# Largest value over the partitions: from a transpose and a product on TensorE to a reduction on GpSimd, and biases turned by transfers

## The chip, the cores and the metric

The kernel runs on one core of a Trainium2 chip. The core has TensorE (matmuls, from SBUF into PSUM banks), VectorE, ScalarE, GpSimd, and SyncE, whose queue (SP) issues most DMA transfers. Each engine works through its own queue in order, and engines wait for each other by semaphores. The metric is the device time of one execution, in microseconds (us). Before the change the median of 3 runs is 686.72 us (685.91 to 687.05).

## The reference, cut to what matters

The input x has 2048 rows of 1024, in bf16. Two branches read it, and a gate mixes their outputs.

```
qkv = x @ wqkv                     # 32 heads of 32; each row attends to 8 rows, 2 apart
a   = softmax(q.k / sqrt(32)) v @ wo
z   = gelu(x @ w_in)               # 3584 columns
z1, z2 = z[:, :1792], layernorm(z[:, 1792:])
g   = w_sp @ z2 + b_sp[:, None]    # w_sp is 2048 x 2048, b_sp has 2048 entries
b   = (z1 * g) @ w_out
out = s * a + (1 - s) * b          # s = sigmoid(x . gate_w)
```

## The kernel before, in words

All matmuls are in 16 bits, most of them 128x128 weights against 512 moving columns (L302, L617, L802, L829, L920, L1048, L1137). Their order on TensorE is: the second half of x @ w_in (`z2_tile`, L302), the q, k, v blocks (`plain_rows`, L617, then `row_pair`, L637), the rest of the second half (L302 again), the first half of x @ w_in (L802), w_sp @ z2 (`g_chunk`, L829, then `seven_products`, L920), and the products with w_out and wo (`mix_pair`, `attn_pair` and `both_pairs`, L1048, L1127, L1137). The attention itself is elementwise work on VectorE (L342 to L398), laid beside the matmuls. ScalarE copies most results out of the PSUM banks (L307, L623, L805, L833). The tile called `ps` rotates through all eight banks, and the small results `po` and `pt` of this change take banks from the same rotation.

The order of the work is written out by hand. The class `Beat` counts the matmul columns issued so far and turns them into a time; functions are put on a list with a due time (`beat.at`) and are issued when the count of columns reaches it. So the order in each engine's queue is fixed when the kernel is built.

Parts of four products (`row_pair`, `seven_products`, `mix_pair` and `both_pairs`) combine blocks of their factors in fp16 and use seven block products in place of eight. For that, factors are first multiplied by a power of two that brings their largest value to a known size, and results are multiplied by the inverse. The generator `whole_power` (L494) finds such a power for a whole matrix. It is given the largest absolute value of each partition (`top`, 128 x 1) and has three steps, issued at three places of the order:

1. VectorE raises `top` to a floor (L496), cuts it down to its power of two (L497, L498) and writes it as bf16 (L499).
2. TensorE turns the 128 values into one row (L503), and VectorE takes the largest of the row (L504).
3. TensorE multiplies a column of ones with this value spread over 512 columns (L506), which puts it on all partitions. VectorE copies it out (L507), makes the scaling power `up1` and its inverse `back` with integer operations on the exponent (L508 to L512), and multiplies `factors` by the inverse (L513).

`whole_power` is used seven times: for x (first step at L552, the others from L695), q (L595, L716), w_out (`w_steps`, L771 and L1276), wo (`wo_steps`, L1278 and L1277), the attention output (`o_steps`, L1233 to L1236), the first half of z1 * g (`v_steps`, L1227 to L1231) and the second half (`u_steps`, L1296, L1177, L1193). The x scale is read by ScalarE at L561 and by VectorE at L562, in `x_block_sums`.

The rows of the second half of w_sp have powers of their own (`row_powers`, L850), which read the biases of these rows too, one row per partition. So b_sp's second half must lie as `b_in`, 128 partitions by 8. Before the change it is loaded as 8 rows of 128 (`b_row`, L738), transposed on TensorE (`biases`, L786) and copied by ScalarE (L787). The scaled biases `b_up` (L866) go the other way: a product with the identity on TensorE (L871), a copy by ScalarE (L873), a store to `bsp_d` in DRAM (L874). Later L877 loads them from there onto all partitions, for `seed` (L775), which puts biases into the banks before the products are added.

Of the kernel before, what the change touches and what calls it, by code (L numbers as in the profile page):

```python
# [2 lines left out]

# [7 lines left out]
F32 = mybir.dt.float32  # L11
BF = mybir.dt.bfloat16
F16 = mybir.dt.float16
I32 = mybir.dt.int32

P = 128
# [41 lines left out]
def kernel(  # L58
# [13 lines left out]
    nc = tc.nc  # L72
# [4 lines left out]
    sm = ctx.enter_context(tc.tile_pool(name="small", bufs=1))  # L77
    psum = ctx.enter_context(tc.tile_pool(name="psum", bufs=8, space=bass.MemoryType.PSUM))
# [15 lines left out]
    bsp_d = dpool.tile([8, P], BF, name="bsp_d")  # L94

    ones = nc.const_aps.tensor(1.0, [P, 512], BF)
# [6 lines left out]
    ident = sm.tile([P, P], BF, name="ident")  # L103
# [15 lines left out]
    expo = sm.tile([P, 8], I32, name="expo")  # L119
    up = sm.tile([P, 8], I32, name="up")  # L120
    down = sm.tile([P, 8], I32, name="down")
    b_row = sm.tile([8, P], BF, name="b_row")
    b_in = sm.tile([P, 8], BF, name="b_in")
    b_up = sm.tile([P, 8], BF, name="b_up")
    w_l1 = sm.tile([P, 7], F32, name="w_l1")
# [1 line left out]
    u_l1 = sm.tile([P, NF], F32, name="u_l1")  # L127
    top = sm.tile([P, 1], F32, name="top")
    top_i = sm.tile([P, 1], I32, name="top_i")
    top_b = sm.tile([P, 1], BF, name="top_b")  # L130
    top_1 = sm.tile([1, 1], BF, name="top_1")
    wo_l1 = sm.tile([P, 4], F32, name="wo_l1")
    o_l1 = sm.tile([P, 32], F32, name="o_l1")
    wo_up = sm.tile([P, 1], I32, name="wo_up")
# [97 lines left out]
    sync = nc.sync  # L232
# [250 lines left out]
    def load_w1(ch):  # L483
        ncol = min(512, FH - 512 * ch)
        sync.dma_start(w1_slots[ch % 2][:, :, 0:ncol], win_v[:, :, 512 * ch:512 * ch + ncol])
# [5 lines left out]
    def load_z1c(c):  # L491
        sync.dma_start(z1c_slots[c][:, 0:12, :].rearrange("p f t -> p (f t)"), z1_d[c, :, 0:12 * 512])

    def whole_power(up1, factors):  # L494
        v = nc.vector
        v.tensor_scalar(top[:], top[:], TINY, None, ALU.max)  # L496
        v.tensor_scalar(top_i[:], top[:].bitcast(I32), 23, None, ALU.logical_shift_right)  # L497
        v.tensor_scalar(top_i[:], top_i[:], 23, None, ALU.logical_shift_left)  # L498
        v.tensor_copy(top_b[:], top_i[:].bitcast(F32))  # L499
        yield  # L500
        po = psum.tile([P, 512], F32, name="po", tag="ps")
        pt = po[0:1, 0:P // 2].bitcast(BF)
        nc.tensor.transpose(pt, top_b[:], ident[:])  # L503
        v.tensor_reduce(top_1[:], pt, AX.X, ALU.max)  # L504
        yield
        nc.tensor.matmul(po[:], ones[0:1, 0:P], top_1[:].to_broadcast([1, 512]), start=True, stop=True)  # L506
        v.tensor_copy(top[:], po[:, 0:1])  # L507
        v.tensor_scalar(top_i[:], top[:].bitcast(I32), 23, None, ALU.logical_shift_right)  # L508
        v.tensor_scalar(up1[:], top_i[:], -1, 254 + TOP, ALU.mult, ALU.add)
        v.tensor_scalar(up1[:], up1[:], 23, None, ALU.logical_shift_left)  # L510
        v.tensor_scalar(back[:], top_i[:], -TOP, None, ALU.add)
        v.tensor_scalar(back[:], back[:], 23, None, ALU.logical_shift_left)  # L512
        v.tensor_scalar(factors, factors, back[:].bitcast(F32), None, ALU.mult)  # L513
        yield
# [30 lines left out]
    for i in range(2, 16):  # L545
        x_sum(i)
        z2_tile(i, 0)
        if i == 8:
            sync.dma_start(z2_d[:], z2[:, 4:8, 0:2, :])
    nc.vector.tensor_reduce(top[:], x_l1, AX.X, ALU.max)  # L550
    x_steps = whole_power(x_up, q_back[:])
    next(x_steps)  # L552

# [26 lines left out]
    def q_sum(k):  # L580
# [8 lines left out]
        beat.on_vector(1.3)  # L589

    q_steps = whole_power(q_up, q_back[:])

    def q_first_step():
# [141 lines left out]

    load_w1(0)
    load_w1(1)
    sync.dma_start(b_row[:], bass.AP(tensor=B_b_sp.tensor, offset=B_b_sp.offset + 1024, ap=[[P, 8], [1, P]]))  # L738
    for i in range(2, 16):
        z2_tile(i, 1)  # L740
        if i == 3:
# [26 lines left out]
    for g in range(NG):  # L768
        beat.at(beat.now + 6.0 + 10.0 * g, lambda g=g: turn_wo(g))
    w_steps = whole_power(w_up, omg[:])  # L770
    beat.at(beat.now + 72.0, lambda: (nc.vector.tensor_reduce(top[:], w_l1[:], AX.X, ALU.max), next(w_steps)))  # L771

    seeded = []

    def seed(v):  # L775
        ps = psum.tile([P, 512], F32, name="ps", tag="ps")
        nc.scalar.copy(ps[:], v)
        seeded.append(ps)
# [2 lines left out]
        seed(bsp_bc[:, 1024:1536])  # L781
        seed(bsp_more)

    def biases():
        pt = psum.tile([P, 8], BF, name="pt", tag="ps")
        nc.tensor.transpose(pt[:], b_row[:], ident[0:8, 0:8])  # L786
        nc.scalar.copy(b_in[:], pt[:])  # L787

    for f in range(NF):
        ch = f // 4  # L790
        w1 = w1_slots[ch % 2]
        if f % 4 == 0 and ch in (1, 2):
            load_w1(ch + 1)
        z1s = z1s_slots[f % 4]
        if f == 4:
            biases()
        for c in range(4):
            if 4 * f + c >= 4 * NF - AHEAD:
                seed(bsp_bc[:, 0:512])
            ps = psum.tile([P, 512], F32, name="ps", tag="ps")  # L800
            for kt in range(KT):
                nc.tensor.matmul(ps[:], w1[:, kt, (f % 4) * P:(f % 4 + 1) * P], xT[:, kt, 512 * c:512 * (c + 1)],  # L802
                                 start=(kt == 0), stop=(kt == KT - 1))
            keep = f > 11 and c < 2
            nc.scalar.activation(z1c_slots[c][:, f, :] if keep else z1s[:, c, :], ps[:], ACT.Gelu_apprx_tanh)  # L805
            beat.run(KT * 512)
        c0 = 2 if f > 11 else 0
        beat.at(beat.now + (3.0 if f < 11 else 0.0), lambda f=f, c0=c0, z1s=z1s: sync.dma_start(
            z1_d[c0:4, :, f * 512:(f + 1) * 512].rearrange("c p t -> p c t"), z1s[:, c0:4, :]))
        if f == 12:  # L810
            load_z1c(0)
# [55 lines left out]
        TT(omg[:, 8:16], omg[:, 8:16], down[:].bitcast(F32), ALU.mult)  # L867

    def scaled_biases():
        pt = psum.tile([8, 512], F32, name="pt", tag="ps")  # L870
        nc.tensor.matmul(pt[:].rearrange("p (a t) -> p a t", a=4), b_up[:],  # L871
                         ident[:].rearrange("p (a t) -> p a t", a=1).to_broadcast([P, 4, P]), start=True, stop=True)
        nc.scalar.copy(b_row[:], pt[:, 0:P])  # L873
        sync.dma_start(bsp_d[:], b_row[:])  # L874

    def load_scaled_biases():
        sync.dma_start(bsp_bc[:, 1024:S], bass.AP(tensor=bsp_d.tensor, offset=bsp_d.offset, ap=[[0, P], [1, 1024]]))  # L877
# [388 lines left out]
    beat.at(t0 + 41.5, lambda: row_powers(4, 8))  # L1266
    beat.at(t0 + 42.5, row_powers_back)
    beat.at(t0 + 64.0, scaled_biases)
    beat.at(t0 + 76.0, load_scaled_biases)
    for k in range(2):  # L1270
# [60 lines left out]
```

## Time and profile before

| what | value |
|---|---|
| median of 3 runs | 686.72 us |
| the profiled execution's own time | 685.84 us |
| its span | 683.7 us |
| L503, transpose, 7 times | 217 ns each, from 39.5 to 588.9 us |
| L506, product, 7 times | 384 ns each, from 42.4 to 595.4 us |
| L786 / L871, biases on TensorE, once each | 174 / 379 ns |
| mean of a 512-column matmul (L829) | 379 ns |
| GpSimd, busy in all | 13.2 us, 9.3 of it in four pows (L470) |

The profile is one execution, taken by the hardware's profiler; its span leaves out some 2 us around the kernel. Rows of a timeline give the start and the length of a group of equal instructions, the engine (PE is TensorE, PEld its weight loads, DVE VectorE, ACT ScalarE, POOL GpSimd, SPq the queue of SP), the line, and what is written from what; in brackets stands how long the engine was idle before it and who ended that. Matmuls overlap: a row's length is longer than the distance from one start to the next.

### The profile page before, as it was taken

The page shows a single profiled execution, that of the slowest core. Times are in us where ns is not written, and L with a number is a line of the kernel's source. Part 1 is how long each engine was busy: PE and PEld are TensorE (multiplying, and loading weights), DVE is VectorE, ACT ScalarE, POOL GpSimd, SP SyncE. Part 2 cuts the span into 40 slices and gives each one's busy share as a digit, 9 for nine tenths or more (in the row PEclk, how much of TensorE's full clock was granted, in tenths as well). Part 3 has the DMA queues.
Part 4 walks back from the last instruction along what each step waited for, and adds up shares of the span by engine and source line. Part 5 has one row for each costly group of instructions (what it writes and reads, how often), then busy time and mean ns, then how long its engine had stood idle before and what let it go on. Part 6 is the DMA issues. An engine that isn't in the chain of part 4 may idle for free.

```text
span 683.7 us, 8977 instructions
## 1 busy us (share of the span) xinstructions
PE 676.1 (99%) x3276; PEld 355.4 (52%) x3327; DVE 564.2 (83%) x701; ACT 417.1 (61%) x767; POOL 13.2 (2%) x45
## 2 busy tenths in 40 slices
PE   9999999999999999999999999999999999999997
PEld 4489666666654565444444444444444444444443
DVE  4649959999999998999998889895578888766653
ACT  4358767655556999758854896426977442232322
POOL 0000000000000022000000000000000000000000
PEclk9999999999999999999999999999999999999999
DMA  8995975544697308899877958919211513222210
GB/s 233 176 206 156 201 206 149 157 127 96 163 234 221 142 1 208 176 285 360 272 297 251 246 204 218 241 46 285 84 57 37 154 37 87 63 68 70 65 45 32
DMA packets 187996, 108.67 MB, mean 159 GB/s; under 512 B 146480, under 2 KB 172592, under 8 KB 187696
## 3 DMA queue, kind: packets, MB, share of 16 engines
q1 hardware_dynamic: 186224, 101.81, 56.6%
q10 hardware_dynamic: 1728, 6.29, 2.6%
q8 instruction: 26, 0.43, 0.3%
q14 instruction: 18, 0.15, 0.1%
HBM read 59.51 MB, written 34.41 MB: 137 GB/s over the span
## 4 chain that ended last, share of the span: by engine, by line
PE 97%; DMA 1%; issue 0%; SPq 0%; ACT 0%; DVE 0%; DVEq 0%
PE ps L617 16%; PE ps L829 14%; PE ps L802 14%; PE ps L302 14%; PE ps L920 12%; PE ps L1048 12%; PE ps L637 7%; PE ps L1137 6%; PE ps L1127 1%; DMA arena<-in_B_w_in_dram 1%; PE po L506 0%; SPq L523 0%; PE po L503 0%; SPq L521 0%; SPq L519 0%
## 5 line engine op out<-in xcount | busy, mean ns | idle before, releaser
L617 PE MATMUL ps<-arena 128*128 128x512 bf16 (+1 forms) x637 | 115.6, 337 | 0.2
L302 PE MATMUL ps<-arena 128*128 128x512 bf16 (+1 forms) x501 | 97.3, 352 | 0.7
L829 PE MATMUL ps<-arena 128*128 128x512 bf16 x439 | 97.3, 379 | 0.5
L617 PEld LDWEIGHTS <-arena 128*128 128x128 bf16 x640 | 83.1, 144 | 27.8 <-issue 0.5
L802 PE MATMUL ps<-arena 128*128 128x512 bf16 x439 | 96.6, 379 | 0.5
L1048 PE MATMUL ps<-arena 128*128 128x512 f16 (+1 forms) x380 | 91.2, 379 | 0.5
L920 PE MATMUL ps<-arena 128*128 128x512 f16 (+1 forms) x385 | 84.9, 379 | 0.6 <-issue 0.3
L302 PEld LDWEIGHTS <-arena 128*128 128x128 bf16 x512 | 50.2, 98 | 47.5 <-issue 0.6
L802 PEld LDWEIGHTS <-arena 128*128 128x128 bf16 x448 | 43.7, 98 | 52.4
L348 DVE TENSOR_TENSOR arena<-arena 128x8192 bf16<-128x8192 bf16 x16 | 70.7, 4420 | 0.2
L391 DVE TENSOR_TENSOR arena<-arena,att_A 128x8192 bf16<-128x8192 bf16 x16 | 70.7, 4419 | 0.0
L829 PEld LDWEIGHTS <-arena 128*128 128x128 bf16 x448 | 43.4, 98 | 52.5 <-issue 0.5
L1048 PEld LDWEIGHTS <-arena 128*128 128x128 f16 (+1 forms) x392 | 38.3, 98 | 46.1
L920 PEld LDWEIGHTS <-arena 128*128 128x128 bf16 (+1 forms) x392 | 38.0, 98 | 46.1 <-issue 0.5
L623 ACT CAST arena<-ps 128x512 bf16<-128x512 f32 (+1 forms) x80 | 38.9, 527 | 32.2 <-PE ps L617 30.6
L351 DVE TENSOR_TENSOR arena<-arena 128x4096 bf16<-128x4096 bf16 (+1 forms) x32 | 56.2, 1755 | 0.8
L637 PE MATMUL ps<-arena 128*128 128x512 f16 (+1 forms) x224 | 52.4, 379 | 0.0
L307 ACT ACTIVATE arena<-ps 128x512 bf16<-128x512 f32 x64 | 34.2, 537 | 27.8 <-PE ps L302 27.8
L1137 PE MATMUL ps<-arena 128*128 128x512 f16 (+3 forms) x200 | 50.3, 375 | 0.1
L1117 DVE SCALAR_TENSOR_TENSOR arena<-ps,g_s,arena 128x512 bf16<-128x512 f32 (+2 forms) x33 | 24.0, 734 | 28.7 <-ACT arena L1169 19.9
L805 ACT ACTIVATE arena<-ps 128x512 bf16<-128x512 f32 x56 | 32.1, 600 | 19.8 <-PE ps L802 17.5
L637 PEld LDWEIGHTS <-arena 128*128 128x128 f16 (+1 forms) x224 | 32.2, 144 | 16.1
(204 smaller groups left out, 779.1 us busy)
## 6 DMA issues: line engine op xcount, KB each, us to landing
arena<-k_d SPq DMA_DIRECT2D x8, 960.0 KB, 7.3
arena<-v_d SPq DMA_DIRECT2D x8, 960.0 KB, 6.5
arena<-in_A_wqkv_dram SPq DMA_DIRECT2D x24, 256.0 KB, 5.1
z_d<-arena SPq DMA_DIRECT2D x12, 512.0 KB, 7.6
arena<-q_d SPq DMA_DIRECT2D x8, 512.0 KB, 3.9
o_d<-arena SPq DMA_DIRECT2D x4, 1024.0 KB
arena<-in_B_w_in_dram SPq DMA_DIRECT2D x4, 1024.0 KB
arena<-in_B_w_sp_dram ACTq DMA_DIRECT2D x8, 512.0 KB, 6.7
```

Source lines behind the costliest of these rows:

```text
L302: nc.tensor.matmul(ps[:, 0:N], xT[:, kt, i * P:(i + 1) * P], w2[c][:, kt, 0:N], start=(kt == 0), stop=(kt == KT - 1))
L348: TT(prod.rearrange("p (w j c) -> p w j c", w=W, j=8, c=C), in0, in1, ALU.mult)
L351: return lambda: TT(pv[:, :, 0:half], pv[:, :, 0:half], pv[:, :, half:2 * half], ALU.add)
L391: TT(prod.rearrange("p (w j d h) -> p w j d h", w=W, j=8, d=DH, h=HG), in0, in1, ALU.mult)
L617: nc.tensor.matmul(ps[:, n0:n1].rearrange("p (t c) -> p t c", c=C), lhsT, wgt[:, pos0:pos1, kt, :], start=(kt == 0), stop=(kt == KT - 1))
L623: nc.scalar.copy(slot[:, j % 4, n0:n1], ps[:, n0:n1])
L637: nc.tensor.matmul(dst[:].rearrange("p (t c) -> p t c", c=C), lhs(k), rhs[:, :, k, :], start=first and k == 0, stop=k == 3, skip_group_che ...
L802: nc.tensor.matmul(ps[:], w1[:, kt, (f % 4) * P:(f % 4 + 1) * P], xT[:, kt, 512 * c:512 * (c + 1)], start=(kt == 0), stop=(kt == KT - 1))
L829: nc.tensor.matmul(ps[:], z2[:, f, i, :], wsp[:, i, :, :].rearrange("p a t -> p (a t)"), start=False, stop=(i == 15), skip_group_check=True)
L920: nc.tensor.matmul(dst[:], lhs[:, k, :], rhs(k), start=False, stop=k == 7, skip_group_check=True)
L1048: nc.tensor.matmul(dst[:], lhs[:, j, :], rhs(j), start=first and j == 0, stop=j == 6, skip_group_check=not first)
L1137: nc.tensor.matmul(dst, lhs[:, k, :], rhs[:, k, :], start=first and k == 0, stop=k == 3, skip_group_check=not first)
```

## The change

In `whole_power` the maximum over the partitions is now one GpSimd instruction, `partition_all_reduce`, issued in the first step. It reads `top` in float32 and writes the largest value to all partitions of `top_all`. The bf16 cut, the transpose, the row maximum, the product and the copy go. The three steps stay where they were, the second of them empty, and the last one starts from `top_all`.

The biases are turned by the transfers: `b_in` is loaded in its final layout, element by element, and the scaled biases are stored to `bsp_d` element by element from `b_up`. `biases` and its call go, and `scaled_biases` is one DMA.

```diff
-    b_row = sm.tile([8, P], BF, name="b_row")
...
-    top_b = sm.tile([P, 1], BF, name="top_b")
-    top_1 = sm.tile([1, 1], BF, name="top_1")
+    top_all = sm.tile([P, 1], F32, name="top_all")
...
         v.tensor_scalar(top[:], top[:], TINY, None, ALU.max)
-        v.tensor_scalar(top_i[:], top[:].bitcast(I32), 23, None, ALU.logical_shift_right)
-        v.tensor_scalar(top_i[:], top_i[:], 23, None, ALU.logical_shift_left)
-        v.tensor_copy(top_b[:], top_i[:].bitcast(F32))
+        nc.gpsimd.partition_all_reduce(top_all[:], top[:], P, bass_isa.ReduceOp.max)
         yield
-        po = psum.tile([P, 512], F32, name="po", tag="ps")
-        pt = po[0:1, 0:P // 2].bitcast(BF)
-        nc.tensor.transpose(pt, top_b[:], ident[:])
-        v.tensor_reduce(top_1[:], pt, AX.X, ALU.max)
         yield
-        nc.tensor.matmul(po[:], ones[0:1, 0:P], top_1[:].to_broadcast([1, 512]), start=True, stop=True)
-        v.tensor_copy(top[:], po[:, 0:1])
-        v.tensor_scalar(top_i[:], top[:].bitcast(I32), 23, None, ALU.logical_shift_right)
+        v.tensor_scalar(top_i[:], top_all[:].bitcast(I32), 23, None, ALU.logical_shift_right)
         v.tensor_scalar(up1[:], top_i[:], -1, 254 + TOP, ALU.mult, ALU.add)
...
-    sync.dma_start(b_row[:], bass.AP(tensor=B_b_sp.tensor, offset=B_b_sp.offset + 1024, ap=[[P, 8], [1, P]]))
+    sync.dma_start(b_in[:], bass.AP(tensor=B_b_sp.tensor, offset=B_b_sp.offset + 1024, ap=[[1, P], [P, 8]]))
...
-    def biases():
-        pt = psum.tile([P, 8], BF, name="pt", tag="ps")
-        nc.tensor.transpose(pt[:], b_row[:], ident[0:8, 0:8])
-        nc.scalar.copy(b_in[:], pt[:])
...
-        if f == 4:
-            biases()
...
     def scaled_biases():
-        pt = psum.tile([8, 512], F32, name="pt", tag="ps")
-        nc.tensor.matmul(pt[:].rearrange("p (a t) -> p a t", a=4), b_up[:],
-                         ident[:].rearrange("p (a t) -> p a t", a=1).to_broadcast([P, 4, P]), start=True, stop=True)
-        nc.scalar.copy(b_row[:], pt[:, 0:P])
-        sync.dma_start(bsp_d[:], b_row[:])
+        sync.dma_start(bass.AP(tensor=bsp_d.tensor, offset=bsp_d.offset, ap=[[1, P], [P, 8]]), b_up[:])
```

More of the change, by code (lines that the diff above doesn't have):

```diff
@@ L5 @@
 import concourse.tile as tile
-from concourse import bass_utils, mybir
+from concourse import bass_isa, bass_utils, mybir
 from concourse._compat import with_exitstack
```

## The prediction

> **What bounds the kernel now.** I read the page first: the engines' shares, the row of slices, the chain that ended last.
>
> ```profile
> span 683.7 us, 8977 instructions
> PE 676.1 (99%) x3276; PEld 355.4 (52%) x3327; DVE 564.2 (83%) x701; ACT 417.1 (61%) x767; POOL 13.2 (2%) x45
> PE   9999999999999999999999999999999999999997
> PEclk9999999999999999999999999999999999999999
> PE 97%; DMA 1%; issue 0%; SPq 0%; ACT 0%; DVE 0%; DVEq 0%
> ```
>
> TensorE is busy in every slice, at full clock, and is 97% of the chain. Busy alone proves little, since a matmul's row (379 ns) overlaps the next. So I went to the view of waits, for PE:
>
> ```profile
> PE pw L101 <- PEq L1315: 0.8, 1, 0.8
> PE ps L920 <- issue: 0.3, 2, 0.2
> ```
>
> In the whole run TensorE waits 1.1 us: the start, and two short stops. Then the timeline, to get the beat: one undisturbed stretch, then a stretch with two of the products that the change deletes.
>
> ```profile
> 402.72 10.74 PE L829 MATMUL ps<-arena 128*128 128x512 bf16 x49
> ...
> 424.30 2.75 PE L829 MATMUL ps<-arena 128*128 128x512 bf16 x12
> 426.99 0.38 PE L871 MATMUL pt<-ident,b_up 128*8 128x512 bf16 x1
> 427.30 3.63 PE L829 MATMUL ps<-arena 128*128 128x512 bf16 x16
> 430.85 0.22 PE L503 MATMUL po<-ident,top_b 128*1 128x128 bf16 x1
> 431.00 2.33 PE L829 MATMUL ps<-arena 128*128 128x512 bf16 x10
> ```
>
> 49 matmuls end 10.74 us after the first starts, the last lasting 0.38: (10.74 - 0.38)/48 = 0.216 us a matmul. The reader is to see that TensorE never leaves this beat except around the small products. So TensorE's instruction stream is the time, and what leaves the stream leaves the time, as long as nothing else becomes late.
>
> **TensorE, what is removed.** The price of a small product is the excess over the beat. L871: from 424.30 to 427.30 pass 3.00 us for 12 matmuls, 12 x 0.216 = 2.59, so 0.41. L503: from 427.30 to 431.00 pass 3.70 us for 16, 16 x 0.216 = 3.46, so 0.24, and the next matmul starts another 0.01 late: 0.25. The same reading, with narrow windows of the timeline, gives for the others:
> - transposes at L503: five among 512-wide matmuls at 0.25 = 1.25; two (x and q scale) among L617 at 0.30 = 0.60;
> - products at L506: five at 0.42 = 2.10; two at 0.47 = 0.94;
> - bias transpose L786: 0.21; bias product L871: 0.41.
>
> Together 5.5 us, all on the bound engine. No work beside it hides it.
>
> **VectorE.** Each of the seven searches loses five instructions (L497, L498, L499, L504, L507), which follow each other every 0.19 to 0.20 us: 0.95 us each, 6.6 us in all. It also loses stalls on TensorE, as in the first search:
>
> ```profile
> 35.23 0.15 DVE L496 TENSOR_SCALAR top<-top 128x1 f32<-128x1 f32 x1
> ...
> 39.78 0.28 DVE L504 TENSOR_REDUCE top<-po 1x1 bf16<-1x128 bf16 x1 [3.83 <-PE po L503]
> 42.87 0.16 DVE L507 COPY top<-po 128x1 f32<-128x1 f32 x1 [2.81 <-PE po L506]
> ```
>
> VectorE is not the bound, so I book none of this. It matters as cover: VectorE gets lighter where TensorE gets faster.
>
> **GpSimd, what is added.** One reduction over 128 partitions x 1 element per search; the trace has none. Lower end: a memset of 128x1, 0.10 us. Upper end: the longest pow (L470, 128x4), 2.98 us. The pow rows explain their own spread:
>
> ```profile
> 239.23 1.22 DVE L351 TENSOR_TENSOR arena<-arena 128x2048 bf16<-128x2048 bf16 x1
> ...
> 239.41 1.92 POOL L470 TENSOR_TENSOR rstd<-var,cm 128x4 f32<-128x4 f32 x1 [28.88 <-DVE var L469]
> ...
> 263.25 2.28 DVE L397 TENSOR_TENSOR arena<-arena 128x4096 bf16<-128x4096 bf16 x1
> ...
> 263.42 2.98 POOL L470 TENSOR_TENSOR rstd<-var,cm 128x4 f32<-128x4 f32 x1 [4.87 <-DVE var L469]
> ```
>
> The fold ends at 240.45 and the pow at 241.33; the fold ends at 265.53 and the pow at 266.40. The pow finishes 0.87 to 0.88 us after the VectorE instruction it started beside. I take 0.9 us, the net pow, as nearest, plus up to 4.42 us (the longest VectorE row) held up: 1 to 5.3 us from the maximum per partition to the result.
>
> The Trainium skill ("SBUF — State Buffer", SBUF: two separate sides) calls the port pair of VectorE and GpSimd an exclusive lock held for a whole instruction. The trace agrees in the direction that the pow rows show; in the other direction it would take up to 0.9 us per search from VectorE, seven times 6.3 us, about what VectorE saves.
>
> **The new wait.** The VectorE instruction at the old L508 now waits for GpSimd, with all of VectorE's queue behind it. From the end of L496 to the start of L507, where VectorE used to go on, the trace allows 7.5 us (x), 22.8 (q), 60 (w), 36 (wo), 15.2 (o), 12.0 (v) and 29 (u). The estimate of 1 to 5.3 us fits in the shortest. GpSimd's own queue holds only memsets and the pows, and none runs when a maximum becomes ready; the memset closest behind one is at 349.6, 11.5 us after w's maximum.
>
> **Biases by transfers.** Loading b_in now moves 1024 pieces of 2 bytes, and the store to bsp_d too. The row of the gate vector has just that shape (128 partitions x 8 elements of 2 bytes):
>
> ```profile
> L733 SPq DMA_DIRECT2D arena<-in_gate_w_dram x1: 368/368/368, 208.8 to 208.8; - x1
> ...
> DMA to landing us min/median/max: 4.2/4.2/4.2
> ```
>
> Issue 0.37 us (L738, which it replaces, took 0.90), landing 4.2. b_in is read first by the row powers over 100 us later: nothing. The store has bounds from 1.5 us to land (the last store of out) to 10.5 (the slowest store to k_d); I take 4.2. SP now reaches it at 427.2, since it used to stand 3.8 us for ScalarE's copy at L873; the reload that waits for it went out at 442.8. 15 us cover it, and the ScalarE copies (0.16 and 0.25 us) vanish. Transposing loads behind it in SP's queue go out up to 3.8 us earlier. Cost 0.
>
> **Sum.** The profiled execution took 685.8 us (span 683.7 and 2.1 around it). 685.8 - 5.5 = 680.3. The median of the three runs, 686.7, lies 0.9 above that execution; carried over, 686.7 - 5.5 = 681.2, my forecast.
>
> **Rivals.**
> 1. *Part of the gain comes back as waits.* Between 110 and 460 us VectorE is busy 332 of 350 us, so data may come just in time. The tightest place I found: the third product of the first seven (L949) starts at 462.3 and needs the sum of L897, which VectorE ends at 461.3; margin 1.0 us. TensorE gains 2.9 us before VectorE's last wait for it (1.65 us at 430.8) and 0.7 us after. For: busy VectorE. Against: at 430.8 VectorE waited for TensorE's results, so it follows; from there to L897 it loses 0.4 us of its own, leaving 0.3 of a 1.0 margin used. If half of the 5.5 returns here: 684.0.
> 2. *Slower: GpSimd's answer is late in the first search.* ScalarE needs x_up at 44.3 (L561), in the same queue that empties TensorE's banks:
>
> ```profile
> 44.28 3.73 ACT L561 ACTIVATE arena<-arena,x_up 128x4096 bf16<-128x4096 bf16 x1
> 47.91 1.44 ACT L623 CAST arena<-ps 128x256 bf16<-128x256 f32 x5
> ```
>
>    L561 keeps ScalarE 3.7 us, then five waiting casts follow at once, and TensorE did not stop. Eight banks, each filled by 8 matmuls of 0.109 us, hold 7.0 us, so up to 3.3 more are in reserve. A search of T us stalls TensorE by T - 7.5 - 3.3. It eats the gain at T = 16 and makes the kernel slower beyond 18. At T = 20: x loses 9.2, and VectorE comes 8 us late at v and 5 at o, of which I count half, 6.5: 681.2 + 15.7 = 697. For: a routine that the trace has not shown. Against: the longest GpSimd row is 2.98 us, and GpSimd is idle from 1.5 to 83 us, so it could prepare ahead. The Trainium skill ("GPSIMD Engine Reference", Instruction dispatch) says that the first call to newly loaded code costs about 6 us without a row; by that x would come at 35.4 + 6 + 0.9 = 42.3, still in time, and the sum would stay.
> 3. *All is given back*, by such an answer at T near 16, or by the store of the biases landing after 442.8 and holding SP: 686.7.
> 4. *More than the sum*: VectorE's lost stalls and the 0.3 us of TensorE's stops add up to 1.5 us: 679.7.
>
> **Chances.** Forecast (680.3 to 682.2) 0.60; rival 1 (682.2 to 685.3) 0.17; rival 4 0.05; rival 3 0.06; rival 2 0.12. The range leaves out rivals 2 and 3 and the tail of 4: 679.6 to 685.3. This kernel's measurement can tell about 0.2%, 1.4 us, from no change. Faster by more: 0.60 + 0.17 + 0.05 = 0.82; within: 0.06; slower: 0.12.
>
> **What would show it.** Right: no TensorE rows at 503, 506, 786, 871; the waits of PE still near 1 us; seven reductions on GpSimd of 0.1 to 5.3 us; VectorE not waiting for GpSimd at w, wo, u. Wrong: PE waits of several us on VectorE or ScalarE after 36 us (rival 2 at 44 to 55, rival 1 from 460), a reduction result over 7.5 us after its maximum, or L877 going out later than 443.

## The result, and the profile after

The changed kernel is slower: its median is 703.25 us (700.86 to 711.26, 6 runs) against 686.44 us (685.91 to 687.05, 6 runs), a ratio of 1.0262 (95% interval 1.0217 to 1.0308). The forecast of 681.2 us and its range up to 685.3 us are both missed.

The profiled execution is the longest of the changed kernel's runs, 711.26 us. Its page, in the lines that answer to those of before (engine totals, TensorE's slices and granted clock, the chain that ended last):

```profile
span 709.5 us, 8982 instructions
PE 679.4 (96%) x3311; PEld 356.3 (50%) x3311; DVE 557.7 (79%) x666; ACT 416.9 (59%) x765; POOL 21.3 (3%) x52
PE   5999999999999999999999999935999999999997
PEclk9999999999999999999999999968999999999999
PE 93%; DVE 2%; SPq 1%; issue 1%; DMA 1%; ACT 0%; POOL 0%; DVEq 0%; POOLq 0%
```

Before, every slice of TensorE was a 9. Now there are two holes: the first slice (5), and the 27th and 28th (3 and 5, 461 to 497 us). A slice is 17.7 us. The view of waits for TensorE names both:

```profile
PE ps L899 <- ACT ps L767: 11.7, 1, 11.7
PE ps L899 <- DVE arena L876: 7.2, 1, 7.2
PE pt L316 <- POOL ident masks.py:199: 6.6, 1, 6.6
PE pw L101 <- PEq L1294: 0.8, 1, 0.8
```

Three new waits, 25.5 us, against 1.1 us in all before. (Lines move: L899 is L920 before, L767 the copy in `seed`, L876 the sum L897 before, L316 the transposes of x that open the kernel.)

**The hole at the start.** The timeline of GpSimd and TensorE:

```profile
9.83 0.28 POOL masks.py:199 TENSOR_SCALAR_AFFINE_SELECT ident<-ident 128x128 bf16<-128x128 bf16 x1 [8.76 <-issue]
...
10.17 1.86 PE L316 MATMUL pt<-ident,arena 128*128 128x128 bf16 x16 [6.57 <-POOL ident masks.py:199]
```

and the same instruction before:

```profile
1.10 0.29 POOL masks.py:199 TENSOR_SCALAR_AFFINE_SELECT ident<-ident 128x128 bf16<-128x128 bf16 x1
```

GpSimd makes the identity matrix that TensorE's first transposes need. The instruction is as short as before (0.28 us), but it starts at 9.83 in place of 1.10 us, after 8.76 us in which GpSimd waits for nothing that the profile shows ("issue"). The transposes start 6.56 us later (3.61 before), and the first matmuls after them come 0.43 us apart, twice the beat, for some 2 us: the last matmul of the first stage starts at 44.22 in place of 36.60 us, 7.62 later.

**The hole in the middle.** SP's queue, after and then before:

```profile
435.09 0.58 SPq L853 DMA_DIRECT2D bsp_d<-b_up  x1
435.78 34.02 SPq L487 DMA_TRANSPOSE arena<-wsp_d  x4
469.90 0.53 SPq L856 DMA_DIRECT2D arena<-bsp_d  x1
```

```profile
430.98 0.30 SPq L874 DMA_DIRECT2D bsp_d<-b_row  x1
431.38 11.35 SPq L489 DMA_TRANSPOSE arena<-wsp_d  x4
442.83 0.54 SPq L877 DMA_DIRECT2D arena<-bsp_d  x1
```

The four transposing loads behind the element-wise store take 34 us to issue in place of 11, and the biases' reload goes out at 469.90 in place of 442.83. In the trace's completion events the store itself lands at 461.8, 26.7 us after its issue; the reload, 8 us later still, stood behind the transposing loads in SP's queue. Two waits elsewhere follow. The view of waits for VectorE has a load of w_sp, the view of the tile `bsp_d` has ScalarE's copy in `seed`:

```profile
DVE arena L872 <- DMA arena<-wsp_d: 20.5, 1, 20.5
```

```profile
  ACT ps L767: 17.3, 1
```

TensorE then waits for `seed` (11.7 us), and after it for L876, which VectorE reaches late because of L872 (7.2 us).

All DMA traffic was slow meanwhile. The window from 440 to 460 us (busy time of each engine, granted clock, DMA share, GB/s), after and then before:

```profile
440.00:460.00 20.00, 20.00 (x95) 9.09 (x93) 11.99 (x9) 3.69 (x7) 0.00 (x0) 1.00 1.32 38
```

```profile
440.00:460.00 20.00, 19.89 (x92) 8.88 (x92) 19.76 (x25) 4.53 (x8) 0.00 (x0) 1.00 0.42 88
```

38 GB/s in place of 88, at a higher DMA share: the queues were occupied, not empty. After the hole the granted clock stays below full speed (the third number from the end):

```profile
475.00:483.00 8.00, 5.70 (x16) 1.77 (x15) 7.86 (x16) 3.81 (x7) 0.00 (x0) 0.74 0.08 19
483.00:500.00 17.00, 12.09 (x45) 5.00 (x46) 13.23 (x17) 4.09 (x8) 0.00 (x0) 0.80 0.65 205
```

**The ledger of the profiled execution**, by where the same matmul starts or ends in both traces. TensorE is 7.62 us late at the end of the first stage; removed products bring that to 4.09 at the end of L829; the wait for `seed` makes it 15.96 at the first of the seven products; at the end it is 25.8 (709.5 - 683.7). Between the last two lie the 7.2 us of the other wait and about 2 us of removed products, so some 4.6 us (25.8 - 16.0 - 7.2 + 2.0) are left, which I put down to the lower clock.

**The reductions** were no problem. The line's own view and the longest of the seven, with the VectorE product beside it:

```profile
L495 POOL PARTITION_ALL_REDUCE top_all<-top x7: 352/643/4442, 34.9 to 593.4; - x7
...
  DVE top_i L498: 0.6, 1
```

```profile
422.36 4.44 POOL L495 PARTITION_ALL_REDUCE top_all<-top  x1 [18.47 <-DVE top L494]
```

```profile
422.18 4.42 DVE L389 TENSOR_TENSOR arena<-arena,att_A 128x8192 bf16<-128x8192 bf16 x1
```

0.35 us at the shortest, 4.44 at the longest, and VectorE waited for one of the seven, 0.6 us.

### The profile page after: what moved, and what is told of

Same layout as the page of the kernel before. It is cut to its first block, busy times and chain, and to the rows that moved or that the text cites. A ratio compares the mean times of both kernels' runs of the same rounds, so it can differ in the third digit from the quotient of the medians.

```text
span 709.5 us, 8982 instructions
## 1 busy us (share of the span) xinstructions
PE 679.4 (96%) x3311; PEld 356.3 (50%) x3311; DVE 557.7 (79%) x666; ACT 416.9 (59%) x765; POOL 21.3 (3%) x52
## 4 chain that ended last, share of the span: by engine, by line
PE 93%; DVE 2%; SPq 1%; issue 1%; DMA 1%; ACT 0%; POOL 0%; DVEq 0%; POOLq 0%
PE ps L607 16%; PE ps L300 14%; PE ps L785 14%; PE ps L812 13%; PE ps L1027 12%; PE ps L899 12%; PE ps L627 7%; PE ps L1116 6%; SPq L487 1%; PE ps L1106 1%; DMA arena<-wsp_d 1%; DVE arena L872 0%; DVE arena L876 0%; DVE arena L395 0%; DVE arena L874 0%
## 5 line engine op out<-in xcount | busy, mean ns | idle before, releaser
L607 PE MATMUL ps<-arena 128*128 128x512 bf16 (+1 forms) x640 | 114.9, 336 | 0.0
L899 PE MATMUL ps<-arena 128*128 128x512 bf16 (+1 forms) x392 | 89.6, 392 | 18.9 <-ACT ps L767 11.7
L300 PE MATMUL ps<-arena 128*128 128x512 bf16 (+1 forms) x512 | 99.1, 356 | 0.0
L1027 PE MATMUL ps<-arena 128*128 128x512 f16 (+1 forms) x392 | 92.8, 379 | 0.0
L899 PEld LDWEIGHTS <-arena 128*128 128x128 bf16 (+1 forms) x392 | 39.2, 100 | 69.3 <-issue 17.4
L627 PE MATMUL ps<-arena 128*128 128x512 f16 (+1 forms) x224 | 52.4, 379 | 0.0
```

The costliest lines, as they stand in the source:

```text
L300: nc.tensor.matmul(ps[:, 0:N], xT[:, kt, i * P:(i + 1) * P], w2[c][:, kt, 0:N], start=(kt == 0), stop=(kt == KT - 1))
L607: nc.tensor.matmul(ps[:, n0:n1].rearrange("p (t c) -> p t c", c=C), lhsT, wgt[:, pos0:pos1, kt, :], start=(kt == 0), stop=(kt == KT - 1))
L627: nc.tensor.matmul(dst[:].rearrange("p (t c) -> p t c", c=C), lhs(k), rhs[:, :, k, :], start=first and k == 0, stop=k == 3, skip_group_che ...
L899: nc.tensor.matmul(dst[:], lhs[:, k, :], rhs(k), start=False, stop=k == 7, skip_group_check=True)
L1027: nc.tensor.matmul(dst[:], lhs[:, j, :], rhs(j), start=first and j == 0, stop=j == 6, skip_group_check=not first)
```

## The experiments

My theory after the traces: two separate losses. A reduction anywhere in the program delays GpSimd's identity matrix at the start, and the element-wise store of the biases holds up the DMA traffic of the middle. The rivals put the loss in the searches themselves, or in the element-wise load. All ratios are against the kernel before, run on the same chip.

### The change in three parts: e1_search, e2_store, e3_load

e1_search has the change's `whole_power` and leaves the biases as before. The other two have one transfer each:

```diff
# e2_store: scaled_biases becomes
+        sync.dma_start(bass.AP(tensor=bsp_d.tensor, offset=bsp_d.offset, ap=[[1, P], [P, 8]]), b_up[:])
# e3_load: biases() and b_row's load go
+    sync.dma_start(b_in[:], bass.AP(tensor=B_b_sp.tensor, offset=B_b_sp.offset + 1024, ap=[[1, P], [P, 8]]))
```

> The seven searches on GpSimd alone; both turns of the biases stay on TensorE. Theory A (two separate losses: the first GpSimd code exchange holds up the identity matrix at the start, +7.6 us by the stage ends of the two traces; the 2-byte store of the scaled biases holds up the writes to DRAM, +14.7; the removed products give 5.5 back): 686.4 - 4.9 + 7.6 = 689.1 us, TensorE waiting 6.6 us for the identity and nowhere else. Rival B (the searches make the loss in the middle too, for instance by late answers or because everything stands some us later): about 703 us, with the waits near 465 us still there.

> The kernel before with one edit: the scaled biases are stored from b_up element by element (2 bytes each), without the product on TensorE. Theory A: 686.4 - 0.4 + 14.7 = 700.7 us, the reload of the scaled biases and the transposing loads of the last quarter of w_sp 15 to 25 us later than before. Rival B (the store is innocent, it only looked late because other things were): 686.0 us.

> The kernel before with one edit: the biases are loaded element by element into b_in, without the transpose on TensorE and its copy. Theory A (reads of 2 bytes are cheap, only writes to DRAM are not): 686.4 - 0.2 = 686.2 us. Rival C (2-byte transfers cost in both directions, and the issue of this load, 3.2 us instead of 0.9, holds SP's queue up): 688 to 690 us.

| kernel | median us | before, us | ratio (95%) |
|---|---|---|---|
| e1_search | 687.22 | 686.23 | 1.0013 (1.0004 to 1.0023) |
| e2_store | 699.65 | 686.23 | 1.0201 (1.0174 to 1.0227) |
| e3_load | 686.44 | 686.23 | 1.0003 (0.9989 to 1.0016) |

TensorE's waits in e1_search and then in e2_store:

```profile
PE pt L317 <- POOL ident masks.py:199: 5.9, 1, 5.9
PE pw L101 <- PEq L1306: 0.8, 1, 0.8
```

```profile
PE ps L916 <- DVE arena L893: 6.8, 1, 6.8
PE ps L916 <- DVE arena L902: 2.1, 1, 2.1
```

Each part has one of the two holes and not the other, so theory A held and rivals B and C fell. Its sizes were a little high: 700.7 us for e2_store, and 689.1 for e1_search, where the start cost less than the 7.6 us taken from the changed kernel. In e1_search TensorE is 6.92 us late at the end of the first stage and 1.99 at the last product: the removed products give back 4.93 us, which is the 4.89 that the prediction counted for the searches. The loss at the start eats all of it. In e2_store the store costs 13.4 us (699.65 - 686.23), although a product of 0.41 us is gone. The load of the biases costs nothing that can be measured, although it also moves 1024 pieces of 2 bytes, 2 bytes apart in DRAM: it reads DRAM, and the store writes it.

### Presence alone: e4_unused

The kernel before, with one reduction that nobody reads:

```diff
+    top_all = sm.tile([P, 1], F32, name="top_all")
...
+            nc.gpsimd.partition_all_reduce(top_all[:], cm05[:, 0:1], P, bass_isa.ReduceOp.max)
             next(u_steps)
```

> The kernel before plus one GpSimd reduction near the end (at 566 us) whose result nobody reads; nothing is removed. Theory A (its presence alone makes GpSimd exchange code ahead of the identity matrix): 686.4 + 7.6 = 694.0 us, the whole loss before 37 us. Rival D (the cost of a reduction is where it runs): 686.4 us, start unchanged.

Measured: 692.24 us, ratio 1.0082 (1.0064 to 1.0100). GpSimd's identity matrix and its reduction, then TensorE's wait:

```profile
8.72 0.28 POOL masks.py:199 TENSOR_SCALAR_AFFINE_SELECT ident<-ident 128x128 bf16<-128x128 bf16 x1 [7.65 <-issue]
...
409.93 0.38 POOL L1298 PARTITION_ALL_REDUCE top_all<-cm  x1 [6.08 <-issue]
```

```profile
PE pt L319 <- POOL ident masks.py:199: 5.5, 1, 5.5
```

The line stands at the place of 566 us in the program, but the reduction needs nothing that is made late, so GpSimd runs it at 409.93, as soon as its queue reaches it. That is still 401 us behind the identity matrix, yet the identity matrix is late at 8.72 us, and 5.71 of the 6.1 us by which the span is longer lie before 42.3 us. So it isn't the reduction's work that costs, but that the program has one: theory A held, at 692.24 in place of its 694.0, and rival D fell.

In every trace here that has a reduction and an affine select, GpSimd stands still for 7.65 to 8.76 us ahead of the affine select; in those without a reduction, or without the affine select (g1_ident, below), it doesn't. Two records that set GpSimd's code stand ahead of the affine select, before and after the change alike:

```profile
masks.py:199 POOLq MODIFY_POOL_CONFIG  x2: 12/12/12, 1.0 to 1.0; - x2
```

```profile
masks.py:199 POOLq MODIFY_POOL_CONFIG  x2: 12/12/12, 1.1 to 1.1; - x2
```

The records themselves are equally short (12 ns each). What differs is the time from the second of them to the affine select: 0.06 us before, 8.7 us after. In e4_unused two more such records stand ahead of the reduction, at 404.0 and 404.1, and there too GpSimd stands still, for 6.08 us, though the reduction waits for no other engine. That GpSimd has to fetch code at these places when a program needs two kinds of it, and finds it in place when it needs one, is what I conclude; the trace shows the standstill and not the fetch.

### The identity matrix by another engine: g1_ident

Searches on GpSimd as in the change, biases as before, and the identity matrix made by VectorE from a column of row numbers, its transpose and a comparison:

```diff
-    make_identity(nc, ident[:])
+    nc.gpsimd.memset(ident[:], 0.0)
...
+    nc.vector.memset(col[:, 0:1], 0.0)
+    for n in (1, 2, 4, 8, 16):
+        nc.vector.tensor_scalar(col[:, n:2 * n], col[:, 0:n], float(n), None, ALU.add)
+    nc.vector.transpose(turned[:], col[:])
+    for b in range(4):
+        r = slice(32 * b, 32 * b + 32)
+        nc.vector.tensor_tensor(ident[r, r], col[r, :], turned[r, :], ALU.is_equal)
```

> The searches on GpSimd, the biases as before, and the identity matrix made by VectorE (doubling adds, a 32x32 transpose, four comparisons), so that GpSimd's first instruction with code to load is the first search. Theory A: the start as before (identity ready near 3 us), so 686.3 - 4.9 = 681.4 us. Rival J (the exchange still costs at the start, or the first search comes late for want of its code): 684 to 688 us.

Measured: 681.19 us (681.05 to 681.79), ratio 0.9930 (0.9913 to 0.9946). It is the fastest kernel of this study and beats both. All its waits of TensorE:

```profile
PE ps L309 <- DMA arena<-in_B_w_in_dram: 1.3, 2, 1.0
PE pw L100 <- PEq L1314: 0.8, 1, 0.8
```

VectorE ends the matrix at 2.93 us, ahead of x's arrival. With the affine select gone, GpSimd's start costs nothing, and the first reduction starts at 34.98 us, when its maximum is ready. The seven searches come in time, so rival J fell. The gain, 4.98 us (686.17 - 681.19), is the 4.89 us of the fourteen small products that the prediction had priced.

### What makes the store slow: f1 to f8

Each of these is the kernel before with one extra store beside its own, ahead of the four transposing loads, into a spare DRAM buffer that nobody reads. So nobody waits for it, and what it costs is what it does to others. Only the layout differs:

```diff
+        sync.dma_start(bass.AP(tensor=spare_d.tensor, offset=spare_d.offset, ap=[[1, P], [P, 8]]), b_up[:])          # f1: 2 bytes apart
+        sync.dma_start(bass.AP(tensor=spare_d.tensor, offset=spare_d.offset, ap=[[32, P], [32 * P, 8]]), b_up[:])   # f2: 64 bytes apart
+        sync.dma_start(spare_d[:], b_up[:])                                                                        # f3: rows of 16 bytes
+        sync.dma_start(bass.AP(tensor=spare_d.tensor, offset=spare_d.offset, ap=[[16, P], [2, 8]]), b_up[:])        # f4: 4 bytes apart
```

> The kernel before, biases as before, plus one more store that nothing reads or waits for until the end: b_up element by element, 1024 pieces of 2 bytes, packed into 2 KB of DRAM as in the change, right behind the store of the biases in SP's queue. Theory E (the packed 2-byte writes themselves hold up the other writes to DRAM, those of w_sp's rows among them): about as slow as the store alone, 697 to 700 us. Rival F (they only land late, and the loss is SP's wait for them ahead of the reload): 686.3 us.

> As the run before, with the same 1024 pieces of 2 bytes each 64 bytes from the next, over 64 KB of DRAM. Theory G (many small writes into the same few bytes of DRAM get in each other's way): 686.5 us, no stall near 460 us. Rival H (any write of 2 bytes is slow, wherever it goes): 697 to 700 us.

> As the two runs before, with b_up stored as it lies: 128 pieces of 16 bytes, packed into 2 KB. Theories E and G: an eighth of the pieces into the same 2 KB, at most 1.7 us of loss, 686.3 to 688. Rival I (what counts is that 2 KB take writes from many partitions at all, not how many pieces): 697 us.

> The kernel before plus one more store that nothing reads: b_up as 1024 pieces of 2 bytes, every other 2 bytes of a 4 KB piece of DRAM, so that the 8 pieces of one partition stand together in 32 bytes (in the change, neighbours in DRAM come from 128 different partitions). Theory K (it is neighbours coming from different partitions, thus by different DMA engines at once, that get in each other's way): landing near the 4.5 us of the spread store, 686.3 us. Rival L (it is the density alone, 8 to 16 pieces in 32 bytes): landing about 10 us, 690 to 694 us.

f5_quiet takes f1's store to a quiet place, from ScalarE's queue at 247.7 us, with the identity matrix as its data:

> The kernel before plus the packed store (1024 pieces of 2 bytes into 2 KB, source a part of the identity matrix, nothing reads it) issued from ScalarE's queue near 245 us, where the DMA engines are nearly idle. Theory E (the pieces are slow by themselves): still 10 us or more to land, and no loss of time, as no other write to DRAM is due: one look of 686 to 688 us. Rival M (they are slow only beside the stores of w_sp): landing in 4.5 us.

f6 and f7 are f2 at 32 and 16 bytes apart; f8 stores one column alone, 128 pieces into 256 bytes:

```diff
+        sync.dma_start(bass.AP(tensor=spare_d.tensor, offset=spare_d.offset, ap=[[1, P], [P, 1]]), b_up[:, 0:1])    # f8
```

> The kernel before plus one more store that nothing reads: b_up as 1024 pieces of 2 bytes, each 32 bytes from the next (32 KB of DRAM). Theory P (what makes the packed store slow is many pieces inside one stretch of 32 to 64 bytes of DRAM, each to be merged into it in turn; 8 or more make it as slow as packed): with 2 pieces in 64 bytes, landing 4.5 to 7 us and 686.3 us. Rival Q (one piece in 64 bytes is free, any second one costs as much as 31): landing near 15 us, 691 to 698.

> As the run before, with 16 bytes from one piece to the next (16 KB): 4 pieces in 64 bytes. Theory P: landing between 4.5 and 10 us, 686 to 690 us. Rival Q: landing near 15 us, 691 to 698.

> As the packed store, but only the first column of b_up: 128 pieces of 2 bytes into 256 bytes of DRAM. Theory R (the time grows with the number of pieces, (16.0 - 4.5)/1024 = 0.011 us each): landing 4.5 to 6 us, 686.3 us. Rival S (the pieces that share a stretch are the price, and a few stretches are as bad as many): landing over 8 us.

| kernel | pieces | apart | landing us | median us | ratio (95%) |
|---|---|---|---|---|---|
| f1_packed | 1024 of 2 B | 2 B | 16.0 | 698.42 | 1.0174 (1.0159 to 1.0189) |
| f4_same | 1024 of 2 B | 4 B | 15.4 | 693.38 | 1.0104 (1.0071 to 1.0137) |
| f8_one | 128 of 2 B | 2 B | 15.1 | 698.38 | 1.0205 (1.0152 to 1.0257) |
| f7_gap16 | 1024 of 2 B | 16 B | 4.6 | 686.47 | 1.0009 (0.9995 to 1.0024) |
| f6_gap32 | 1024 of 2 B | 32 B | 4.9 | 686.41 | 1.0000 (0.9990 to 1.0009) |
| f2_spread | 1024 of 2 B | 64 B | 4.5 | 686.32 | 1.0002 (0.9992 to 1.0011) |
| f3_rows | 128 of 16 B | 16 B | 4.5 | 686.31 | 1.0003 (0.9994 to 1.0012) |

The window from 436 to 446 us, in which the transposing loads run, for f1, f8, f7 and then for the kernel before (the last number is GB/s):

```profile
436.00:446.00 10.00, 10.00 (x48) 4.56 (x47) 9.85 (x9) 2.38 (x5) 0.00 (x0) 1.00 1.31 32
```

```profile
436.00:446.00 10.00, 10.00 (x48) 4.55 (x47) 9.85 (x9) 2.38 (x5) 0.00 (x0) 1.00 1.41 21
```

```profile
436.00:446.00 10.00, 10.00 (x47) 4.57 (x47) 9.85 (x9) 2.38 (x5) 0.00 (x0) 1.00 1.10 230
```

```profile
436.00:446.00 10.00, 10.00 (x47) 4.58 (x47) 9.85 (x9) 2.25 (x4) 0.00 (x0) 1.00 1.05 202
```

An unread store of 2 KB (f1), and one of 256 bytes (f8), bring all traffic of the core from 202 to 32 and 21 GB/s. SP's queue and TensorE's wait in f1:

```profile
432.45 21.16 SPq L490 DMA_TRANSPOSE arena<-wsp_d  x4
```

```profile
PE ps L922 <- DVE arena L899: 7.6, 1, 7.6
```

21.16 us for the four transposing loads in place of 11.35, and the same wait for the same VectorE sum as in e2_store, although the biases travel by their own, old way. None of the four loads counts on the store's semaphore, either. So what costs is not that something waits for a late store, it is that other transfers stand still: theory E held and rival F fell.

What decides is the layout. The stores 16 bytes apart or more are as free as theories G and P had it, and rivals H, I and Q fell. The number of pieces doesn't: 1024 of them at 16 bytes are free, 128 at 2 bytes cost as much as 1024 (in f8 theory S held, and R, a price for each piece, fell). That neighbours come from different partitions doesn't either: in f4 eight neighbours lie in one partition, and it is slow all the same (theory K fell; the landing of 15.4 us was also longer than rival L allowed). Taking the two orders of the pieces as alike, the limit lies between 4 and 16 bytes for pieces of 2 bytes; 8 was not tried.

f5 was run once, at 685.51 us, so there is no interval for it. By the last of its completion events on record its store lands at 261.6, 14 us after its issue (rival M had 4.5), in a stretch with next to no other traffic; its 1024 packets take at most 9 ns each and are all handed over by 249.3. So the slowness is the store's own, and doesn't come from meeting the transposes. The loads that start while it is under way are held up, f5 first and then the kernel before:

```profile
258.00:262.00 4.00, 4.00 (x26) 2.36 (x25) 4.00 (x1) 4.00 (x13) 0.38 (x4) 1.00 0.76 48
```

```profile
258.00:262.00 4.00, 4.00 (x27) 2.41 (x25) 4.00 (x2) 4.00 (x13) 0.38 (x4) 1.00 0.75 242
```

TensorE waited for none of those loads, and the one time shows no loss: it is the place in f1 that makes the same store cost 12 us.

The Trainium skill ("DMA: Bandwidth & Descriptors", Specifications) says that the DMA engine does a read-modify-write for transfers below 512 bytes. No run here shows that step, and by itself it can't be the cause: f2, f6 and f7 write pieces as small and land in 4.5 to 4.9 us. What happens in the memory when small pieces lie close together is left open.

### Turning the biases without a packed store: g2_hops

g1_ident, and the biases by transfers only: `b_in` loaded element-wise, the scaled biases stored in rows of 16 bytes, read back element-wise into 8 rows, and stored in rows of 256 bytes.

```diff
...
-    beat.at(t0 + 64.0, scaled_biases)
+    beat.at(t0 + 44.5, lambda: sync.dma_start(bup_d[:], b_up[:]))
+    beat.at(t0 + 57.0, lambda: sync.dma_start(b_row[:], bup_d.rearrange("p k -> k p")))
+    beat.at(t0 + 66.0, scaled_biases)
```

> The version that the runs so far point to: searches on GpSimd, identity by VectorE, biases loaded element by element, and the scaled biases turned without TensorE and without packed 2-byte writes: stored as 128 rows of 16 bytes, read back element by element into 8 rows, stored as 8 rows of 256 bytes. Theory A: all of the 5.5 us, 686.2 - 5.5 = 680.7 us. Rival N (the two more transfers hold SP's queue up near 440 us): 682 us or more.

Measured: 688.65 us (687.33 to 693.39), ratio 1.0044 (1.0022 to 1.0066), 7.5 us above g1_ident where theory A had 680.7. Rival N had the size right, but not the queue. TensorE's wait, and the one in ScalarE's timeline that stands behind it:

```profile
PE ps L909 <- DVE arena L886: 5.6, 1, 5.6
```

```profile
433.85 0.59 ACT L777 CAST ps<-arena 128x512 f32<-128x512 bf16 x1 [6.79 <-DMA b_row<-bup_d]
```

L886 is L897 of before, the sum that the prediction's rival 1 found at a margin of 1.0 us. The element-wise load of `b_row` is issued at 424.15 and lands at 433.4. ScalarE's next store of w_sp rows (L875) counts its landing on the same semaphore as this load, and isn't issued until 433.47; ScalarE stands still behind it for 6.79 us. VectorE then waits 7.9 us for ScalarE's copy (L826), and its attention product starts at 435.65, where g1_ident has it at 429.17; the sum ends 6.1 us later than there. SP's queue was held up as well, as rival N had it: the load of v takes 4.10 us to issue, and the reload of the biases goes out at 445.75 in place of g1_ident's 440.25. But VectorE waited only 0.24 us for the load of v, and TensorE never for the reload. So element-wise reads aren't free everywhere: this one took 9.2 us to land, beside the transposing loads, and something waited for it.

The 0.62 us that TensorE saves are not worth that. In this schedule the bias products on TensorE are better left.

### The change with the start mended: h1_after_ident

The changed kernel whole, with g1's identity matrix.

> The changed kernel with one edit: the identity matrix made by VectorE. Theory A (two losses that add up): 703.3 - 6.5 = 696.8 us by the start's loss in the changed kernel, or 686.2 - 5.5 + 13.4 = 694.1 by the store alone; between 693 and 698, with the wait near 460 us still there. Rival O (the store's stall is worse only because everything stands later): below 690.

Measured: 696.70 us (694.45 to 698.79), ratio 1.0153 (1.0118 to 1.0188). TensorE's waits:

```profile
PE ps L907 <- DVE arena L884: 7.4, 1, 7.4
PE ps L907 <- ACT ps L775: 2.2, 1, 2.2
PE ps L907 <- DVE arena L893: 1.8, 1, 1.8
```

The hole at the start is gone and the one in the middle stays, as theory A had it (rival O fell). By medians the start is worth 6.6 us (703.25 - 696.70; they were not run side by side), between e4's 6.0 and the 7.6 of the profiled execution. What is left, 10.6 us over the kernel before (696.70 - 686.11), is the store's 13.4 us less 2.8: some 2 us less than the 4.9 that the searches give by themselves.

## Why the prediction was wrong

- **What bounds the kernel, and what leaves TensorE: right.** The four kinds of products are gone, and the searches' share was 4.93 us in e1_search's trace and 4.98 us by g1_ident's medians, against 4.89 counted.
- **The reductions: right.** 1 to 5.3 us were expected, 0.35 to 4.44 measured, the longest beside a VectorE product of 4.42 us that it had to sit out, as the pow rows had told. The 7.5 us that the shortest search allows were never used up, and rival 2 (an answer late at the first search) didn't happen.
- **"GpSimd is idle from 1.5 to 83 us, so it could prepare ahead": the first step that failed.** The prediction's list of GpSimd's queue had "only memsets and the pows" and left out the affine select at 1.10 us. It put the preparation of about 6 us at the first search, where it was free; in g1_ident, where nothing else stands in the way, that was right. In the changed kernel a standstill came at the start, between GpSimd's memsets and its affine select, where TensorE's first transposes wait: 7.65 to 8.76 us of standstill, 5.5 to 6.6 us of wait, and 5.7 to 7.6 us lost by the end of the first stage. The prediction looked for what waits behind the added instruction, and not for what an added kind of instruction does to those already ahead of it. The Trainium skill's price ("GPSIMD Engine Reference", Instruction dispatch: about 6 us for the first call to newly loaded code) is near the 6.08 us ahead of the reduction in e4_unused, and below the 7.65 to 8.76 us at the start; the place that the prediction gave it was wrong.
- **"I take 4.2 ... Cost 0" for the store: the second step that failed, and the larger.** The row was that of a load, which reads 1024 pieces of 2 bytes; the same shape as a write landed in 16.0 us in f1_packed and in 26.7 in the changed kernel, above even the upper bound of 10.5. e3_load shows that the read in this layout is harmless. (Its issue, booked at 0.37 us, took 1.81 there and 3.25 in the changed kernel, and that cost nothing.) The cost is also of another kind than the one looked for: 15 us were to cover the landing, but the transposing loads behind it, said to go out "up to 3.8 us earlier", went out up to 27 us later.
- **Rival 3** named the store landing after 442.8 and holding SP, but priced it as giving all back (686.7), not as a loss. **Rival 1** named the tight place: the sum of L897 is what TensorE waited for in e2, f1, g2, h1 and the changed kernel. The cause that it feared, TensorE running ahead, was not it: in g1_ident TensorE runs ahead and waits nowhere for VectorE. VectorE came late through the DMA.
- **What would show it wrong** did: PE waits of several us, and the reload out at 469.9, later than 443.

The sum by measured terms, in medians: searches with the start +1.0 (e1), store +13.4 (e2), load +0.2 (e3) make 14.6 of the 16.8 us (703.25 - 686.44). The 2.2 us between are open. In the changed kernel the store is issued 7 us later and takes longer (26.7 us against 20 in e2_store and 16 in f1_packed), and its runs spread over 10 us; what sets the length of such a store wasn't settled.

## What to carry to other kernels

A price taken from a row has to come from the same direction: a write of many small pieces is not a read of them, and a slow one is paid by whatever else uses the DMA at that time. When an engine gets a kind of instruction that the program didn't have, look at what that engine does first, and at who waits for it, not only at the place of the new instruction. A change in several parts is worth taking apart: here the searches on GpSimd, with the identity matrix made elsewhere, give 0.7% by themselves (681.19 us), the store is the part to drop, and the load gave nothing that could be measured.

## What the runs showed of the hardware that was not expected

- One reduction over the partitions anywhere in a program delayed GpSimd's affine select at the start by 7.65 to 8.76 us, even 401 us ahead of the reduction.
- The reduction of 128 partitions x 1 took 0.35 us undisturbed; a transpose and a product on TensorE had taken from 35.38 to 42.87 us for the same in the first search, and VectorE waited 6.64 us of that time for TensorE.
- A store of 2-byte pieces 2 or 4 bytes apart, added to the kernel before, took 14 to 16 us to land, for 256 bytes as for 2 KB, and brought the core's DMA traffic from 202 to 21 to 46 GB/s; 16 bytes apart it took 4.6 us and cost nothing. An element-wise read from packed DRAM cost nothing (e3_load); one into 8 partitions, beside the transposing loads, took 9.2 us to land (g2_hops).
- Around and after the 18.9 us of waiting in the middle of the changed kernel, TensorE's granted clock was 0.74 to 0.80 from 475 to 500 us; about 4.6 us of that execution's time beyond the waits go with it.
